# The last group's k load moves from ScalarE's DMA queue to SyncE's, in a fused attention and SwiGLU kernel

## The chip, the cores and the metric

The kernel runs on one core of one Trainium2 chip. The metric is the device time of one execution in microseconds (us). The engines are named as in the profile: PE (TensorE, with PEld its weight loads), DVE (VectorE), ACT (ScalarE), POOL (GpSimd) and SP (SyncE). SPq and ACTq are the DMA issues in the instruction streams of SP and ACT.

## The reference

A decayed linear attention over 4 batches, 8 heads, 768 positions and a head size of 64 is followed by a SwiGLU block of 512 by 1536. In short:

```python
for b in range(nb):                       # blocks of 64 positions
    intra = (qb @ kb.T * Dmask) @ vb      # per batch and head; Dmask = lam ** (i - j), causal
    inter = (qb * lam_pow) @ kv_state
    out[:, :, sl] = intra + inter
    kv_state = lam_block * kv_state + (kb * rev_pow).T @ vb
x = out.transpose(0, 2, 1, 3).reshape(B * S, H * D)      # 3072 x 512
result = (silu(x @ w_gate) * (x @ w_val)) @ w_out        # 3072 x 512
```

All inputs and the output are float32 in memory; the kernel multiplies in bfloat16.

## The kernel before, in words

The order of the work on every engine is written out by hand; there is no scheduler. The attention is cut into 12 groups (0 to 11), each of 256 positions of one batch with all heads. Two groups make one token tile `t` (0 to 5) for the SwiGLU block, so attention of later groups runs between the SwiGLU steps of earlier tiles. Groups 6 to 11 share one form, which matters here:

- `load_group(g)` loads k (`kraw`, four DMAs), q (`qraw`, four) and v (two DMAs), 512 KB each, in this order.
- `cast_scaled(g)` makes the bfloat16 tile `qk`: ACT casts k (L279), DVE multiplies q by its decay (L281), and then SP issues one transposing DMA from `qk` into `qkt` (L269), which waits for both.
- `v_scale(g)` multiplies v by its decay on POOL (L256), into `v_s`.
- `scores(g)` (PE L374, masks on DVE L379) needs `qkt`; `upd_mm(g)` (PE L406) needs `v_s` and `qk`; `inter` (L500) and `intra` (L513) make the attention output.
- `attend(g)` puts them together on PE: `inter(g)`, `upd_mm(g + 1)`, `scores(g + 1)`, `intra(g)`.

In the stage around the change, token tile 3 runs its SwiGLU steps (L564 gate on PE, silu on ACT L569, L582 value on PE, product on DVE L586). In step 6 of that tile the plan calls `cast_scaled(10)` and then `load_group(11)`. `attend(8)` and `attend(9)` follow steps 5 and 10. Then comes `out_units(2)`, the output projection of tile 2 (PE L802), which is made of seven products per half, in the order p1, p7, p6, p2, p5, p4, p3. ACT copies the result of p1 (L813) and p7 (L817) out, DVE adds (L827) what p6 left in a bank to the copy of p7, and p5 reuses that bank; after p5 DVE adds once more (L831), before p3 uses the bank again. A list of small jobs, handed out between the products by a fixed count, puts `cast_scaled(11)` behind p1 and four subtractions on DVE (`x_combo`, L693) behind p7, p2 and p5. `scores(11)` and `upd_mm(11)` come in the unit after it, `ffn_unit(4, 0)` (PE L712, DVE L754).

A load that ACT or SP issues stands in that engine's order like any other instruction: what is behind it in the stream waits until it is issued.

Of the kernel before, what the change touches and what calls it, by code (L numbers as in the profile page):

```python
# [19 lines left out]
@with_exitstack  # L20
def kernel(
    ctx: ExitStack,
    tc: tile.TileContext,
    q: bass.AP,
    k: bass.AP,
    v: bass.AP,
    lam: bass.AP,
    moe_w_gate: bass.AP,
    moe_w_val: bass.AP,
    moe_w_out: bass.AP,  # L30
    out: bass.AP,
):
    nc = tc.nc
    with tc.manual_schedule():
        _body(ctx, tc, nc, q, k, v, lam, moe_w_gate, moe_w_val, moe_w_out, out)


def _body(ctx, tc, nc, q, k, v, lam, moe_w_gate, moe_w_val, moe_w_out, out):
# [70 lines left out]
    def load_fp32(g, eng, src, what, h0=0, h1=H):  # L109
        if (what, g) not in st:  # L110
            st[(what, g)] = (v_pool if what == "v" else raw_pool).tile(
                [128, H, 2 * D], FP32, name=what, tag="v" if what == "v" else "raw")
        t = st[(what, g)]
        if g < NAT0:
            eng.dma_start(out=t[:, h0:h1], in_=gsrc(src, g, h0)[:, 0:h1 - h0])
            return
        b, i = groups[g]
        base = src.offset + b * H * S * D + i * 2 * BLK * D
        parts = [(0, 128, False)] if what == "v" else [(0, M, False), (M, M, True)]
        for s in range(2):  # L120
            for p0, n, rev in parts:
                eng.dma_start(
                    out=t[p0:p0 + n, :, s * D:s * D + D],
                    in_=bass.AP(tensor=src.tensor,
                                offset=base + (H - 1) * S * D * rev + (p0 + s * BLK) * D,
                                ap=[[D, n], [-S * D if rev else S * D, H], [1, D]]))
# [134 lines left out]
    def load_group(g, parts="kqv"):  # L261
        for src, what in ((k, "kraw"), (q, "qraw"), (v, "v")):
            if what[0] in parts:
                load_fp32(g, nc.scalar if what == "kraw" and g in KACT else nc.sync, src, what)

# [54 lines left out]
                        op=ALU.mult)  # L320


    KACT = (11,)
    later = []

    def run_later(n):
# [939 lines left out]
```

## Time and profile before

| what | value |
|---|---|
| median of 3 runs | 218.8 us (218.75 to 219.83) |
| the profiled execution | 219.09 us, span 217.3 us |
| granted PE clock | 1.00 |
| PE busy | 209.8 us, 97% of the span |
| DVE, ACT, POOL busy | 149.0, 129.0 and 91.5 us |
| k loads on SP | 28 issues (20 of 128 KB, 4 of 256 KB, 4 of 512 KB), 128 KB landing after 3.2 us (median) |
| k loads on ACT | 4 of 128 KB, 4.7 us |

The span runs from the first to the last instruction of one execution; the execution's own time is 1.8 us longer. Rows of a timeline give the start, the duration, the engine, the line, the operation with its output and inputs, the count, and in brackets the idle time before it with what ended it. In the chain of work that ended last each row is a start, a length and the work. The time to landing of a DMA is counted from the start of its issue. A releaser in brackets is inferred from semaphores; where the engine named had been done for long, it was another, often a DMA.

### The profile page before, as it was taken

To read this page: it belongs to the slowest core of one execution; us is meant where nothing else is said; L and a number is where in the kernel's file an instruction comes from. 1 tells how busy PE (TensorE), PEld (TensorE's weight loads), DVE (VectorE), ACT (ScalarE), POOL (GpSimd) and SP (SyncE) were. 2 spreads that over 40 slices of the span, in tenths; PEclk is the share of its full clock that TensorE was granted. 3 is DMA by queue.
4 is the path that set the end of the run, shared out by engine and by line. 5 is a ranking of instruction groups with operands and counts; after the bars stand their busy time and mean duration, and the time that the engine had idled before them with its cause. 6 is when DMAs were issued, how large, how long until landed. Compare 5 with 4: busy or idle time off the path is not lost.

```text
span 217.3 us, 6851 instructions
## 1 busy us (share of the span) xinstructions
PE 209.8 (97%) x2797; PEld 154.5 (71%) x2801; DVE 149.0 (69%) x267; ACT 129.0 (59%) x280; POOL 91.5 (42%) x126
## 2 busy tenths in 40 slices
PE   8879999999999999999999998999999999999994
PEld 3557455888887548866654544888888888888883
DVE  1763447576678799765387979896797379961760
ACT  6778577566545144638367566755882766646522
POOL 6675645927599050777852325410650022200200
PEclk9999999999999999999999999999999999999999
DMA  6999999999997877989779999572000400005014
GB/s 186 346 355 383 374 352 310 264 277 226 386 254 160 198 205 177 242 189 232 189 162 212 204 204 210 128 203 89 5 5 3 193 0 3 0 0 196 0 51 145
DMA packets 88320, 39.76 MB, mean 183 GB/s; under 512 B 57698, under 2 KB 83938, under 8 KB 88290
## 3 DMA queue, kind: packets, MB, share of 16 engines
q1 hardware_dynamic: 84978, 38.22, 65.8%
q10 hardware_dynamic: 3312, 1.11, 2.0%
q8 instruction: 22, 0.36, 0.7%
q14 instruction: 8, 0.07, 0.1%
HBM read 28.31 MB, written 6.29 MB: 159 GB/s over the span
## 4 chain that ended last, share of the span: by engine, by line
PE 90%; ACT 3%; DVE 2%; POOL 2%; issue 1%; POOLq 1%; DVEq 0%
PE bank L802 21%; PE bank L564 20%; PE bank L582 19%; PE bank L712 15%; PE bank L602 5%; PE bank L513 3%; PE bank L500 2%; PE bank L406 1%; PE bank L348 1%; DVE ssb L355 1%; PE bank L310 1%; POOL v_s L256 1%; PE bank L374 1%; PE bank L180 1%; ACT sil L739 1%
## 5 line engine op out<-in xcount | busy, mean ns | idle before, releaser
L586 DVE TENSOR_TENSOR h<-sil,bank 128x256 bf16<-128x256 bf16 (+1 forms) x67 | 35.0, 533 | 27.8 <-PE bank L582 20.5
L564 PE MATMUL bank<-xt,wg_sb 128*128 128x256 bf16 (+1 forms) x276 | 52.6, 315 | 0.0
L582 PE MATMUL bank<-xt,wv_sb 128*128 128x256 bf16 (+1 forms) x276 | 52.4, 314 | 0.0
L569 ACT ACTIVATE sil<-bank 128x256 bf16<-128x256 f32 (+1 forms) x67 | 31.7, 480 | 23.8 <-PE bank L564 19.7
L582 PEld LDWEIGHTS <-wv_sb 128*128 128x128 bf16 x276 | 26.9, 98 | 14.7
L564 PEld LDWEIGHTS <-wg_sb 128*128 128x128 bf16 x276 | 25.9, 98 | 13.4 <-DVE xt L525 0.2
L256 POOL TENSOR_TENSOR v_s<-v,dec 128x512 bf16<-128x512 f32 (+1 forms) x18 | 23.2, 1305 | 27.1 <-DMA v<-in_v_dram 13.9
L742 POOL TENSOR_TENSOR h<-sil,es 128x512 bf16<-128x512 bf16 x6 | 7.0, 1163 | 50.0 <-ACT sil L739 50.0
L802 PEld LDWEIGHTS <-h 128*128 128x128 bf16 x240 | 23.3, 98 | 3.4 <-issue 0.3
L802 PE MATMUL bank<-wo_sb,h 128*128 128x256 bf16 x180 | 21.6, 273 | 0.1
L802 PEld LDWEIGHTS <-hs 128*128 128x128 bf16 x180 | 17.6, 98 | 2.7
L355 DVE TENSOR_TENSOR ssb<-bank,causal 128x512 bf16<-128x512 f32 x24 | 15.4, 684 | 2.7 <-PE bank L348 2.7
L754 DVE TENSOR_TENSOR bank<-bank,es 128x512 f32<-128x512 f32 x12 | 7.8, 694 | 11.4 <-PE bank L712 10.1
L712 PEld LDWEIGHTS <-ws 128*128 128x128 bf16 x144 | 13.8, 97 | 2.3 <-issue 0.2
L802 PE MATMUL bank<-wt,hs 128*128 128x256 bf16 x120 | 15.0, 272 | 0.0
L739 ACT ACTIVATE sil<-bank 128x512 bf16<-128x512 f32 x18 | 10.7, 596 | 7.0 <-POOL h L742 4.6
L461 POOL TENSOR_TENSOR kvf<-kvs,ups 128x256 f32<-128x256 f32 x8 | 5.8, 726 | 19.5 <-ACT ups L428 19.5
L742 DVE TENSOR_TENSOR h<-sil,bank 128x512 bf16<-128x512 bf16 x18 | 12.2, 682 | 1.5 <-ACT sil L739 1.4
L712 PE MATMUL bank<-xs,ws 128*128 128x256 bf16 x96 | 12.8, 272 | 0.0
L525 ACT CAST xt<-bank 128x512 bf16<-128x512 f32 x19 | 11.6, 663 | 2.0 <-PE bank L513 1.5
L461 POOL TENSOR_TENSOR kvf<-kvf,ups 128x256 f32<-128x256 f32 x16 | 12.2, 763 | 0.9
L428 ACT COPY ups<-bank 128x256 f32<-128x256 f32 (+1 forms) x24 | 9.5, 451 | 2.5 <-PE bank L406 2.4
(119 smaller groups left out, 362.0 us busy)
## 6 DMA issues: line engine op xcount, KB each, us to landing
out_dram<-osb SPq DMA_DIRECT2D x22, 256.0 KB, 2.1
v<-in_v_dram SPq DMA_DIRECT2D x18, 256.0 KB, 4.6
woraw<-in_moe_w_out_dram SPq DMA_DIRECT2D x6, 512.0 KB, 8.6
qraw<-in_q_dram SPq DMA_DIRECT2D x24, 128.0 KB, 3.2
wraw<-in_moe_w_gate_dram SPq DMA_DIRECT2D x5, 512.0 KB, 7.4
wraw<-in_moe_w_val_dram SPq DMA_DIRECT2D x5, 512.0 KB, 7.0
kraw<-in_k_dram SPq DMA_DIRECT2D x20, 128.0 KB, 3.2
kraw<-in_k_dram SPq DMA_DIRECT2D x4, 512.0 KB, 6.6
```

What stands on the lines that cost most here:

```text
L256: eng.tensor_tensor(out=st[("vs", g)][:, h0:h1], in0=st[("v", g)][:, h0:h1].rearrange("p h (s d) -> p h s d", s=2), in1=vfac(g, h0, h1), o ...
L355: nc.vector.tensor_tensor(out=ssb[:, h2, 2 * c:2 * c + 2].rearrange("p a s n -> p a (s n)"), in0=sp[(c, h2)].rearrange("p (a x) -> p a x", ...
L461: nc.gpsimd.tensor_tensor(out=o, in0=f, in1=u, op=ALU.add)
L525: fns[r](out=xt[:, g % 2, :, r].rearrange("p h (m s) -> p h s m", s=2) if g < NAT0 else xt[:, g % 2, :, :, r * M:r * M + M], in_=op[r].rea ...
L564: nc.tensor.matmul(gp[:, n0:n1], wg_sb[:, mc, fs], xt[:, g0:g1, mc].rearrange("p g b n -> p g (b n)"), start=(mc == 0 and n0 == 0), stop=( ...
L569: nc.scalar.activation(sil[:, 0:N], gp[:, 0:N], AF.Silu)
L582: nc.tensor.matmul(vp[:, n0:n1], wv_sb[:, mc, fs], xt[:, g0:g1, mc].rearrange("p g b n -> p g (b n)"), start=(mc == 0 and n0 == 0), stop=( ...
L586: nc.vector.tensor_tensor(out=h_sb[:, fc % FH, b0:b1].rearrange("p b n -> p (b n)"), in0=sil[:, 0:N], in1=vp[:, 0:N], op=ALU.mult)
L712: nc.tensor.matmul(o[:, fi * 256:fi * 256 + 256], lhs(i, c, 2 * j + fi), rhs(c), start=(start and fi == 0 and c == 0), stop=(c == KH - 1), ...
L739: nc.scalar.activation(sil[key], src, AF.Silu)
L742: eng.tensor_tensor(out=h_of(half, r), in0=v3(sil[half, r]), in1=v3(src), op=ALU.mult)
L802: nc.tensor.matmul(o, lhs(f), rhs(f), start=(start and f == 0), stop=(f == FH - 1), skip_group_check=True)
```

## The change

`KACT` lists the groups whose k is issued from ACT. It held group 11 and becomes empty, so `load_group(11)` issues all ten DMAs of group 11 from SP. In SP's stream the four k DMAs now stand behind the transposing DMA of group 10, which `cast_scaled(10)` issued, and ahead of the q and v DMAs of group 11. ACT's stream loses four DMA issues, which stood behind its cast of k of group 10; the streams of PE, DVE and POOL keep their order.

```diff
-    KACT = (11,)
+    KACT = ()
```

The one place that reads it, in `load_group`:

```python
load_fp32(g, nc.scalar if what == "kraw" and g in KACT else nc.sync, src, what)
```

## The prediction

> **What bounds the kernel now.** I read the page first: TensorE (PE) is busy 97% of the span at a granted clock of 1.00 throughout, and the chain that ended last is 90% PE. Time can be won or lost only where PE waits. So I took the chain in order of time around group 11's load (126 to 150 us):
>
> ```profile
> 130.72 0.88 PE bank L564 x4
> 131.59 0.08 issue
> 131.67 2.24 POOL v_s L256 x2
> 133.91 0.04 issue
> 133.96 0.38 PE bank L406 x16
> ```
>
> The only foreign link there is GpSimd's `v_scale(10)`. PE's timeline shows what waits: the state update of group 10 (`upd_mm`, L406), against the same step one group earlier, which runs through:
>
> ```profile
> 122.59 0.36 PE L406 MATMUL bank<-v_s,qk 64*64 64x64 bf16 x20
> ...
> 132.77 0.26 PE L406 MATMUL bank<-v_s,qk 64*64 64x64 bf16 x8
> 133.96 0.38 PE L406 MATMUL bank<-v_s,qk 64*64 64x64 bf16 x16 [0.93 <-POOL v_s L256]
> ```
>
> What made GpSimd late stands in the timelines of SyncE's queue (first fence) and ScalarE (second):
>
> ```profile
> 103.78 1.69 SPq L269 DMA_TRANSPOSE qkt<-qk  x1
> ...
> 124.89 2.21 SPq L122 DMA_DIRECT2D v<-in_v_dram  x2
> 129.12 2.99 SPq L269 DMA_TRANSPOSE qkt<-qk  x1
> 132.16 2.66 SPq L122 DMA_DIRECT2D qraw<-in_q_dram  x4
> 134.92 1.20 SPq L122 DMA_DIRECT2D v<-in_v_dram  x2
> 140.36 1.65 SPq L269 DMA_TRANSPOSE qkt<-qk  x1
> ```
>
> ```profile
> 125.70 2.56 ACTq L122 DMA_DIRECT2D kraw<-in_k_dram  x3
> 128.36 1.08 ACT L569 ACTIVATE sil<-bank 128x512 bf16<-128x512 f32 x2 [1.76 <-PE bank L564]
> ```
>
> v of group 10 is issued at 124.89 and 126.49, in the same microseconds as the four k pieces of group 11 on ScalarE's queue (from 124.97). The DMA rows of v, asked one by one, give 5.5 and 5.0 us to landing for these two (so 131.5), and 4.4 us for group 11's second v. GpSimd starts 0.2 us after that landing; its label "PE bank L564" names work long done. The k pieces therefore delay v10. The VectorE (DVE) timeline then shows who needs the loads that the change puts later:
>
> ```profile
> 139.00 1.22 DVE L281 TENSOR_TENSOR qk<-qraw,qdn 128x1024 bf16<-128x1024 f32 x1
> 140.13 1.27 DVE L693 TENSOR_TENSOR xs<-xt 128x512 bf16<-128x512 bf16 x1
> 141.33 0.75 DVE L827 TENSOR_TENSOR bank<-bank,osb 128x256 f32<-128x256 f32 x2
> ...
> 142.52 0.41 DVE L693 TENSOR_TENSOR xs<-xt,xs 128x512 bf16<-128x512 bf16 x1
> ```
>
> L281 scales q11 without waiting. Behind it in order stand L693 and L827, and PE's product p5 of `out_units(2)`, at 141.83, writes the bank that L827 reads. That L827 ends about 141.70, so p5 has some 0.1 us to spare.
>
> **Removed: four issues on ScalarE, 2.7 us** (0.69 and 2.56). They hold ScalarE until 128.26 and two silus come 1.8 us late, but PE has no gap from 123.64 to 132.4. The bank ring covers them: 0.
>
> **Uncovered: v10 comes earlier.** Alone, its two issues take 0.6 each (rows of groups 9 and 11: 0.57 to 0.63), not 1.54. The second starts at 125.5 and lands 4.4 later (group 11's row; groups 6 to 9 show 3.8 to 5.3): 129.9. `v_scale(10)`, 2.23 us, ends at 132.2, before PE asks for it at 132.64. What that is worth: `attend(8)` takes 1.32 us from its first L500 at 122.32 to the next L564 at 123.64; `attend(9)` takes 2.48 (132.37 to 134.85). Difference: **-1.16 us**. The stall can pass to the next in line, the scores of group 10 (L374), which would start at 132.8 and need the transposes of group 10; these land at 134.1 now (129.12 + 5.0). They wait for DVE's L281 of group 10, which waits 0.8 us for q10; its last piece took 3.5 us to land, its first two 3.1. So their issue comes between 128.75 and 129.12; I take 128.9. Their time has two kinds of rows: 1.64 to 1.69 us of issue (78.33, 103.78, 140.36), and 2.73 to 2.99 (89.90, 116.62, 129.12). Before 103.78 the last transfer issued earlier landed 1.3 us after the transposes' start; before 89.90 and 129.12 it landed 3.1 and 3.2 us after (a store, and the last k at 127.66 + 4.7). With k gone, v10 lands some 1.0 us after the start, nearest to 103.78. I take that row: 1.69 of issue, 3.7 to landing, 132.6. The gain stands whole; with 5.0 to landing (133.9) only 0.1 of it is left.
>
> **Moved: k11 behind the transposes, q11 and v11 behind k11.** On SyncE's queue k11's four issues start 1.75 us after the transposes' start (103.78 to 105.53) and take 2.72, so 130.65 to 133.4; the fourth q issue starts 2.04 after the first: 128.9 + 1.75 + 2.72 + 2.04 = 135.4. The same issue now starts at 134.19 and lands 4.2 later; the last q of groups 7 to 10 took 3.2, 4.6, 3.1 and 3.5. I take its own row: q11 is in at **139.6**. DVE, drawn forward with PE, reaches L281 at 139.00 - 1.16 = 137.8 and waits 1.8 us. Then, from landing: 0.13 to start (as at 127.76), 1.13 for L281, 0.33 for L693, 0.37 for the first L827 and 0.1 to PE: p5 starts 2.06 after the landing, at 141.7, against 141.83 now. L693 is put at 0.33 because its 1.27 beside `v_scale(11)` (from 140.06) falls to 0.41 without it, and v11, issued until 138.0, lands after 141. The slow DVE work then falls on the next two L693, ahead of L831; p3 needs L831 4.7 us after q11's landing, and they end at most 4.6 after: 0.
>
> k11's last piece lands near 136.5, before ScalarE's cast at 137.4: 0. Group 11's transposes start about 0.7 us later than now and, at 3.7 to 5.0, land by 146.1; the scores of group 11 run at 147.60: 0. `v_scale(11)` moves from 140.06 to 141.3, used at 152.95: 0. SyncE's next stores wait for data until 144.39: 0.
>
> **Sum.** p5 at 141.7 for 141.83, and behind it PE is the bound to the end: -1.16 + 1.0 = **-0.16 us**. On the profiled 219.09 (span 217.3 and 1.8 around it) that is 218.9; that execution is 0.29 above the median of 218.8, so 218.6 there.
>
> The Trainium skill, "DMA: Bandwidth & Descriptors", section "Queues, rings and completion order", speaks against the change: on each DMA engine a queue's descriptors are consumed in ring order, and ScalarE's queue has a ring of its own. By it k11 can't begin under the transposes, as it could on ScalarE's ring; it names no duration.
>
> **The rivals.**
> *Whole gain*: q11's last piece takes 3.1 us instead of 4.2 and lands at 138.5; p5 is free at 140.6, in time for its advanced start at 140.7. For it: three of the five last-q rows are 3.1 to 3.5. Against: group 11's own 4.2, with the same v behind it. -1.16: 217.6.
> *Late queue, slower*: the transposes' issue stays at 2.99 from 129.12, so q11's fourth issue moves by k11's whole 2.72 to 136.9 and lands at 141.1; p5 starts at 143.2, +1.3 us whatever was won before: 220.1. It decides wherever q11 lands after 139.8. For it: v10 is still in flight when the transposes start, in twice as many pieces of half the size as a store's. Against: the backlog is shorter by 2 us. The same page's section "Issuing engines are not separate DMA queues" says that a second issuing engine saves only the sequencer's time to initiate; by it taking that engine away costs those 2.72 us of issue and wins no transfer rate.
> *Nothing moves*: v10's 5 us came from q10 ahead of it, not from k (group 9's second v took 5.3 without any k beside it), and q11 lands by 139.8: 218.8. Against: v10's first issue took 1.54 and k's third and fourth took 5.7 and 4.7 to land. That the k loads don't move at all is excluded: the built programs differ in these issues alone.
>
> **How the numbers follow.** Forecast 0.48 (-0.9 to +0.6), whole gain 0.14, late queue 0.28 (+0.6 to +2), nothing moves 0.10. About 0.5%, 1.1 us, is what a measurement of this kernel can tell from no change. Faster by that: 0.10 of the whole gain's 0.14. Slower: 0.22 of the late queue's 0.28. Same: 0.68. The range goes from the whole gain, 217.6, to the late queue, 220.2; the forecast's own is 217.9 to 219.4.
>
> **What would show it.** Right: the 0.93 in front of L406 gone, `v_scale(10)` from about 130, the transposes at 128.9 with 1.7 of issue, and a DVE wait of 1 to 2 us for q11 in front of L281, with a PE gap at p5 near 141. Wrong, if `v_scale(10)` still starts at 131.6 (k was not the cause), if PE waits for qkt instead of v_s, or if ScalarE stands at its cast of k11.

## The result, and the profile after

The changed kernel takes a little longer: a median of 219.97 us (218.57 to 223.62, 21 runs) against 218.43 us (217.62 to 219.83, 21 runs) of the kernel before, run in turn with it. The ratio is 1.0049, with a 95% interval of 1.0028 to 1.0070, which is 1.07 us; it leaves three disturbed, slower executions of the changed kernel out, and isn't the quotient of the two medians. The forecast was 0.16 us faster. The profiled execution took 219.38 us, where the one of before had taken 219.09.

The head of the page, and its queues, show that the loads moved and little else did. q10 is ScalarE's queue; it carried 3312 packets and 1.11 MB before:

```profile
span 217.7 us, 6854 instructions
...
q1 hardware_dynamic: 87090, 38.74, 65.8%
q10 hardware_dynamic: 1200, 0.59, 0.9%
```

SyncE's timeline, with start and duration in the first two columns, as in the prediction:

```profile
123.53 2.85 SPq L122 DMA_DIRECT2D v<-in_v_dram  x2
128.91 1.66 SPq L269 DMA_TRANSPOSE qkt<-qk  x1
130.61 2.69 SPq L122 DMA_DIRECT2D kraw<-in_k_dram  x4
133.35 3.67 SPq L122 DMA_DIRECT2D qraw<-in_q_dram  x4
137.12 1.18 SPq L122 DMA_DIRECT2D v<-in_v_dram  x2
```

PE is 0.54 us further ahead here: `attend(8)` begins at 121.78 and not at 122.32. The transposes of group 10 take 1.66 us to issue instead of 2.99; counted from `attend(8)`, they begin at 7.13 instead of 6.80. The k loads stand behind them, and the q loads, which began at 132.16 before, begin at 133.35 and take 3.67 us instead of 2.66. The two v issues of group 10 take 2.85 us, with no k on ScalarE's queue, where they had taken 2.21. GpSimd's timeline has `v_scale(10)` at 129.32, where it was at 131.67, and `v_scale(11)` at 141.96, where it was at 140.06:

```profile
129.32 2.50 POOL L256 TENSOR_TENSOR v_s<-v,dec 128x512 bf16<-128x512 f32 x2 [3.70 <-PE bank L564]
...
141.96 2.45 POOL L256 TENSOR_TENSOR v_s<-v,dec 128x512 bf16<-128x512 f32 x2 [6.39 <-DMA v<-in_v_dram]
```

PE's timeline shows one wait gone and one new:

```profile
132.08 0.42 PE L406 MATMUL bank<-v_s,qk 64*64 64x64 bf16 x24
132.62 0.45 PE L374 MATMUL bank<-qkt 64*64 64x64 bf16 x32
...
138.96 1.47 PE L802 MATMUL bank<-wo_sb,h 128*128 128x256 bf16 x12
141.71 1.47 PE L802 MATMUL bank<-wt,hs 128*128 128x256 bf16 x12 [1.28 <-DVE bank L827]
```

`upd_mm(10)` (L406) no longer stops in the middle, and the scores behind it (L374) wait for nothing. The product p5, the last row, now waits 1.28 us. In the kernel before it had followed p2 without a gap:

```profile
141.83 1.47 PE L802 MATMUL bank<-wt,hs 128*128 128x256 bf16 x12
```

Why it waits is read off the chain of waits, in order of time:

```profile
134.03 1.64 SPq L122
...
136.38 3.25 DMA qraw<-in_q_dram
...
139.76 0.10 DVE qk L281
...
140.90 0.42 DVE xs L693
141.32 0.35 DVE bank L827
...
141.71 4.09 PE bank L802 x36
```

The last piece of q11 is issued at 136.38 and lands 3.25 us later; L281, L693 and L827 follow in DVE's order, and then PE. That is the step that the prediction called the moved one.

A single pair of profiles is not enough here, since executions of one kernel differ by as much as the effect. So the experiments below include three further profiled executions of the kernel before and two of the changed one. All times count from the first L500 of `attend(8)`, except the second column, which is the length of `attend(9)` from its first L500 to the next L564. "End" runs from the issue of SyncE's last store to the end of the span.

| kernel | attend(9) | p5 starts | p3 starts | span ends | end |
|---|---|---|---|---|---|
| before, as predicted from | 2.48 | 19.51 | 22.13 | 94.97 | 2.56 |
| before, three more | 1.33, 2.07, 1.62 | 18.46, 19.09, 18.78 | 21.08, 21.71, 21.40 | 93.9, 94.6, 94.3 | 2.56 each |
| before, mean of four | 1.88 | 18.96 | 21.58 | 94.4 | 2.56 |
| after, three | 1.48, 1.41, 1.28 | 19.93, 19.47, 19.11 | 22.55, 22.41, 22.03 | 95.9, 95.7, 95.35 | 3.03, 3.03, 3.04 |
| after, mean of three | 1.39 | 19.50 | 22.33 | 95.65 | 3.03 |

### The profile page after: what moved, and what is told of

It is laid out like the page before. It is cut to its first block, busy times and chain, and to the rows that moved or that the text cites. A ratio compares the mean times of both kernels' runs of the same rounds, so it can differ in the third digit from the quotient of the medians.

```text
span 217.7 us, 6854 instructions
## 1 busy us (share of the span) xinstructions
PE 209.7 (96%) x2801; PEld 154.1 (71%) x2801; DVE 148.2 (68%) x267; ACT 129.4 (59%) x280; POOL 91.8 (42%) x126
## 4 chain that ended last, share of the span: by engine, by line
PE 78%; DMA 7%; SPq 5%; issue 2%; ACT 2%; DVE 2%; POOL 1%; POOLq 1%; DVEq 0%; ACTq 0%
PE bank L802 18%; PE bank L564 17%; PE bank L582 16%; PE bank L712 15%; PE bank L602 5%; DMA kraw<-in_k_dram 3%; SPq L122 3%; SPq L115 2%; DMA v<-in_v_dram 2%; PE bank L513 2%; PE bank L500 2%; DMA qraw<-in_q_dram 1%; PE bank L406 1%; POOL v_s L256 1%; ACT sil L739 1%
## 5 line engine op out<-in xcount | busy, mean ns | idle before, releaser
L586 DVE TENSOR_TENSOR h<-sil,bank 128x256 bf16<-128x256 bf16 (+1 forms) x67 | 35.1, 533 | 26.6 <-PE bank L582 19.6
L564 PE MATMUL bank<-xt,wg_sb 128*128 128x256 bf16 (+1 forms) x276 | 52.6, 315 | 0.0
L564 PEld LDWEIGHTS <-wg_sb 128*128 128x128 bf16 x276 | 26.0, 98 | 13.4 <-DVE xt L525 0.2
L461 POOL TENSOR_TENSOR kvf<-kvf,ups 128x256 f32<-128x256 f32 x16 | 13.1, 817 | 0.9
L835 ACT COPY osb<-bank 128x256 f32<-128x256 f32 x10 | 3.7, 373 | 12.6 <-PE bank L802 12.6
```

The source lines that it names most:

```text
L461: nc.gpsimd.tensor_tensor(out=o, in0=f, in1=u, op=ALU.add)
L564: nc.tensor.matmul(gp[:, n0:n1], wg_sb[:, mc, fs], xt[:, g0:g1, mc].rearrange("p g b n -> p g (b n)"), start=(mc == 0 and n0 == 0), stop=( ...
L586: nc.vector.tensor_tensor(out=h_sb[:, fc % FH, b0:b1].rearrange("p b n -> p (b n)"), in0=sil[:, 0:N], in1=vp[:, 0:N], op=ALU.mult)
```

## The experiments

The theory after the first look, as the expectations below have it: the stall of 1.16 us at `attend(9)` belongs to every execution of the kernel before; the wait of p5 for q11 is real, and hangs on L281's place in DVE's order; and the program's end costs about half a microsecond more because SyncE's stream holds four more DMAs. The rivals: the stall was long by chance in the one execution shown, q11 is not what p5 waits for, and the longer end is chance. The first part of the theory fell, the other two held.

### The changed kernel again, without an edit

> The changed kernel once more, for a second profiled execution. Theory: PE waits at p5 of the projection of tile 2 for DVE's L827, which stands behind the scaling of q11 (L281), and the size of this wait varies with q11's landing; p5 starts 19.9 us or more after the first L500 of attend(8) (19.5 in the kernel before), and from SP's last store issue to the end of the span it takes 3.0 us (2.6 before). Rival, chance: either of the two is not there again: p5 at 19.5 or the end at 2.6. Time against the kernel before: +0.6 to +1.5 us.

219.47 us (12 runs) against 218.85 (35 runs of before), ratio 1.0028 (0.9998 to 1.0057): +0.6 us, though the interval just takes in no change. The wait of p5 was there, 0.89 us, and "end" was 3.03 as expected. But p5 started at 19.47, below the expected 19.9 and where the rival had it, and p3 started another 0.3 late, for L831. A later execution:

> The changed kernel a third time. Theory: SyncE's issues behind the transposes of group 10 hold one that takes 1.2 to 1.7 us instead of 0.63 (among the fifth to seventh), the fourth q issue starts 7.0 to 7.5 us after the transposes, attend(9) takes 1.3 to 1.7 us, DVE waits 1 to 2.5 us for q11, p5 starts 19.4 to 20.0 us after attend(8)'s first L500, and SP's last six stores to the end take 10.5 to 10.6. Rival (the two executions seen were unlucky ones): no long issue, 6.5 us, p5 at 18.4 to 18.9.

p5 waited 0.63 us and started at 19.11, below what was expected. The long issue was there, but it was the shortest seen, 1.09 us, and the last of the eight; so the fourth q issue started only 6.47 us after the transposes. p3 was again 0.3 late. DVE's timeline of that execution shows where the 0.3 comes from:

```profile
142.05 1.16 DVE L693 TENSOR_TENSOR xt<-xt 128x512 bf16<-128x512 bf16 x1
143.14 1.26 DVE L693 TENSOR_TENSOR xs<-xt,xs 128x512 bf16<-128x512 bf16 x1
144.32 0.74 DVE L831 TENSOR_TENSOR osb<-bank,osb 128x256 f32<-128x256 f32 x2
```

Both L693 lie beside `v_scale(11)`, which ran from 141.88 to 144.11, and take 1.16 and 1.26 us; without it they take 0.41 (last such row of the prediction). L831 stands behind them, and p3 waits for it.

### The kernel before again, without an edit

> The kernel before once more, for a second profiled execution. Theory (the 1.16 us at attend(9) belongs to that kernel, since k11 on ScalarE's queue delays v10): attend(9) takes 2.2 us or more from its first L500 to the next gate product, with a wait of L406 for v_s. Rival (v10's late landing was that execution's alone): attend(9) takes 1.3 to 1.6, v_scale(10) starts before 9.0 us after attend(8)'s first L500, and the removed wait was worth nothing in most executions. p5 at 19.5 by the first and 18.3 to 18.7 by the second; last six stores to the end 10.1 by both.

> The kernel before a third time, to see how often attend(9) waits. Same two readings: 2.2 us or more at attend(9) with a wait for v_s (theory), or 1.3 to 1.6 (rival).

> The kernel before a fourth time. v of group 10 lands 6.2 to 6.7 us after its first issue (with k11 on ScalarE's queue beside it), and what attend(9) takes depends on when that first issue falls: with the issue 1.6 us after attend(8)'s first L500 or less 1.3 to 1.45, with 2.5 us 2.0 to 2.5; p5 between 18.4 and 19.6.

The times were 217.78, 218.33 and 218.81 us. The expectation that the stall is a fixed part of the kernel fell with the first of them. PE's timeline, and under it GpSimd's:

```profile
132.54 0.42 PE L406 MATMUL bank<-v_s,qk 64*64 64x64 bf16 x24
```

```profile
129.94 2.26 POOL L256 TENSOR_TENSOR v_s<-v,dec 128x512 bf16<-128x512 f32 x2 [4.04 <-DMA v<-in_v_dram]
```

Here all 24 matmuls of L406 run in 0.42 us. v10 landed early enough although the k pieces were on ScalarE's queue as always, since SyncE had issued the first v piece 1.58 us after `attend(8)` began and not 2.57. In the other two it was issued at 2.49 and 2.35, and `attend(9)` took 2.07 and 1.62 us. From that issue to the start of `v_scale(10)` the four executions show 6.78, 6.24, 6.40 and 6.13 us. The sum of both is when `v_scale(10)` starts after `attend(8)`, and the stall follows it: 9.35, 7.82, 8.89 and 8.48 us, with 2.48, 1.33, 2.07 and 1.62 us for `attend(9)`. How late v10 is counts for PE only by this sum, and SyncE's offset against PE is a part of it.

### The cast behind p2, in the changed kernel

Here `cast_scaled(11)`, and so L281, stands two jobs further back on DVE, behind the two subtractions and the L827 that p5 needs:

```diff
     trickle[:] = [y for z in TR2 for y in xw[z]]
+    trickle[0:3] = [trickle[1], trickle[2], trickle[0]]
```

> The changed kernel with cast_scaled(11) handed out behind p2 instead of p1, so that DVE's L827 no longer stands behind the scaling of q11. Theory (q11 through DVE's order is what p5 waits for): the wait in front of p5 goes, the 0.93 in front of L406 stays gone, p5 starts 18.4 us after attend(8)'s first L500, and the time is the kernel before's minus 1.2 plus up to 0.5 for the end of the program: -0.6 us, from -1.2 to 0. Rival (what is late is k11 at ScalarE's cast, or the transposes of group 11): a wait of about the same 1.3 us appears at the scores of group 11 or at ScalarE's copies, and the time stays at +0.6 to +1.5 us.

218.71 us (12 runs), ratio 1.0016 (0.9985 to 1.0048). The profiled execution has no wait at p5, which started at 18.68, and p3 at 21.30. DVE's row of L281 and PE's row of p5:

```profile
141.58 1.22 DVE L281 TENSOR_TENSOR qk<-qraw,qdn 128x1024 bf16<-128x1024 f32 x1
```

```profile
142.28 1.47 PE L802 MATMUL bank<-wt,hs 128*128 128x256 bf16 x12
```

L281 is the same work with the same q11, and p5 follows p2 without a gap. So it was L281's place ahead of L827 that handed q11's lateness on to p5. "End" stayed at 3.04.

The gain of 0.6 us that was expected did not come: the ratio allows -0.3 to +1.05 us. Counted from `attend(8)`, the profiled span ended at 94.6, 1.0 earlier than the mean of the changed kernel and 0.2 later than the mean of before. p3 started 0.28 earlier than before, and the longer end took that back. The scores of group 10 waited 0.32 us for their transposes here, which the changed kernel's own three executions do not show. (The execution itself took 219.92 us, 1.2 above its median; most of that arose ahead of `attend(8)`, which began at 123.6.)

### The same edit in the kernel before

> The kernel before with the same move of cast_scaled(11), k11 still on ScalarE's queue. Theory: q11 was no wait there, so nothing is won: the 0.93 in front of L406 stays, p5 at 19.5 us after attend(8)'s first L500, time 0 (within 0.3 us). Rival (the late cast is a gain by itself, by freeing DVE ahead of p5): -0.5 us or more here too.

219.19 us, ratio 1.0020 (0.9993 to 1.0047); `attend(9)` 1.41, p5 18.51, span end 94.0, "end" 2.56. The expected stall at `attend(9)` was not there, which is another miss of the theory that it is fixed: v10 was issued at 1.57 and took 5.49 us in this execution. The times show no gain from the edit where q11 comes early.

### Four small DMAs in the kernel before

The kernel before, with four DMAs of 32 bytes into a tile that nobody reads, on SyncE behind `out_units(2)`. They lengthen SyncE's stream as the change does, and load nothing of weight:

```diff
     out_units(2, many=list(M2))
+    for c in range(4):
+        nc.sync.dma_start(out=pad[0:1, c * H:(c + 1) * H],
+                          in_=bass.AP(tensor=lam.tensor, offset=lam.offset, ap=[[0, 1], [1, H]]))
```

> The kernel before with four more DMAs of 32 bytes in SyncE's stream (into an unused tile), issued where SyncE is idle, so that its stream is as long as in the changed kernel. Theory (the end of the program grows with SyncE's stream): SP's last store issue to the end of the span takes 3.0 us instead of 2.6, and the time is +0.4 to +0.5 us. Rival (the longer end in the changed kernel's profile was chance, or comes from the load itself): 2.6 us, time 0 within 0.2 us.

"End" rose from 2.56 to 3.03, the value of the changed kernel. The last six stores of the kernel before, of the changed one and of this one, in SyncE's timelines:

```profile
207.21 7.86 SPq L808 DMA_DIRECT2D out_dram<-osb  x6
```

```profile
207.11 7.86 SPq L808 DMA_DIRECT2D out_dram<-osb  x6
```

```profile
207.48 7.85 SPq L808 DMA_DIRECT2D out_dram<-osb  x6
```

The stores take the same 7.86 us. From the first of them the span runs on for 10.08 (217.29), 10.56 (217.67) and 10.5 us (218.0). The time was 219.64 us, ratio 1.0028 (0.9993 to 1.0063): in line with half a microsecond, but the interval takes in no change. Nor can its span be used alone, since PE lost 0.8 us ahead of `attend(9)` in that execution, most of it waiting for DVE's L586.

With two DMAs instead of four:

> The kernel before with two more DMAs of 32 bytes in SyncE's stream (four gave 10.5 from the first of the last six stores to the end). If the end grows with each instruction: 10.3. If it is a step at some length of the stream: 10.1 or 10.5.

"End" was 2.47, so the step lies between two and four more DMAs and isn't a price for each. `attend(9)` took 2.48 in this execution, with 0.93 us in front of L406: the long stall does recur. SyncE was not especially late here, with v10's first issue at 2.12, but v10 took 7.19 us, so `v_scale(10)` again started at 9.31.

### Late cast, and a SyncE stream as short as before

The edit of the cast, and the four stores of tile 2 moved from SyncE to ScalarE:

```diff
-        def store(g, r, c0, c1, eng=nc.sync if t >= SY else nc.scalar):
+        def store(g, r, c0, c1, eng=nc.scalar if t == 2 else nc.sync if t >= SY else nc.scalar):
```

> The changed kernel with cast_scaled(11) behind p2, as tried alone, and the four stores of tile 2 issued by ScalarE, which makes SyncE's stream as short as in the kernel before. Theory: no wait at p5 (18.4 to 18.7 us after attend(8)'s first L500) and the program's end back at 10.1 us from the first of SP's last six stores (10.5 to 10.6 with the four issues on SyncE), so from attend(8) to the end of the span 94.2 us or less (95.0 before, 95.9 and 95.7 in the changed kernel); time against the kernel before -0.4 us, from -1 to +0.2. Rival (the end depends on something else than SyncE's stream): 10.5 stays, 94.6.

Half of it held. There was no wait at p5 (18.49), and "end" was back at 2.56 with k of group 11 on SyncE, which shows from the other side that the number of DMAs in SyncE's stream sets it. But the time was 219.99 us, ratio 1.0051 (1.0021 to 1.0082), instead of a gain. PE's timeline has a new wait at the scores of group 11:

```profile
147.26 0.45 PE L374 MATMUL bank<-qkt 64*64 64x64 bf16 x32 [0.78 <-DMA qkt<-qk]
```

The transposes of group 11 were issued at 142.31 and took 4.9 us to land. That takes back 0.78 us. The profiled execution, 218.87 us, ended at 94.8, only 0.4 behind the mean of before; its time is the lowest of its 12 runs, and where the median lost the rest is not shown.

### q11 ahead of k11

In the changed kernel, group 11 alone:

```diff
-        for src, what in ((k, "kraw"), (q, "qraw"), (v, "v")):
+        for src, what in ((q, "qraw"), (k, "kraw"), (v, "v")) if g == 11 else ((k, "kraw"), (q, "qraw"), (v, "v")):
```

> The changed kernel with q11 ahead of k11 in SyncE's queue, both behind the transposes of group 10. Theory (what counts is the last of the loads that cast_scaled(11) takes, since both casts stand ahead of p5's inputs in their engines' order): DVE's wait for q11 falls to 0.5 us or less, ScalarE waits 1.5 to 2.5 us for k11 at its cast, the copies of p7 (L817) stand behind that cast, and PE waits at p5 as long as or longer than now: p5 at 19.9 to 20.6 us after attend(8)'s first L500. Rival (only q's landing counts): p5 at 18.4 to 18.9 and no wait.

One run, 220.49 us. L281 didn't wait for q11, and the expected wait at p5 did not come. ScalarE stood at its cast of k11 instead, for less than the 1.5 to 2.5 us expected:

```profile
140.28 1.05 ACT L279 CAST qk<-kraw 128x1024 bf16<-128x1024 f32 x1 [0.79 <-DMA kraw<-in_k_dram]
```

p5 started at 20.48, inside the range expected, but by luck: PE had waited 0.96 and 0.83 us for DVE's L586 ahead of `attend(9)`, where the order of q11 and k11 had not acted yet. For the same reason what this order is worth can't be read from the run.

### k11 on SyncE, ahead of the transposes

`load_group(11)` leaves its k out, and `load_group(10)` ends with it:

```diff
-                load_fp32(g, nc.scalar if what == "kraw" and g in KACT else nc.sync, src, what)
+                if not (g == 11 and what == "kraw"):
+                    load_fp32(g, nc.sync, src, what)
+        if g == 10:
+            load_fp32(11, nc.sync, k, "kraw")
```

> k11 on SyncE's queue, but ahead of the transposes of group 10 (behind v10). Theory (a load's place in SyncE's one queue decides, not that SyncE issues it): q11's place behind the transposes is the one it has in the kernel before, so its fourth issue starts 5.0 to 6.0 us after the transposes and p5 doesn't wait for it; v10 lands within 5.7 us of its first issue and L406 doesn't wait; the price moves to the transposes, which are issued up to 1.5 us later and land at 12.0 us or later after attend(8)'s first L500, so PE waits for qkt at the scores of group 10, 0.5 to 2 us. Rival (any k on SyncE's queue makes q11 late): DVE waits 1 us or more for q11. The end is 10.5 in both.

One run, 220.95 us, with before at 220.16 beside it. q11 came in time for p5, its fourth issue only 4.39 us behind the start of the transposes, but `attend(9)` took 3.43 us, with PE waiting for the transposes of group 10 (its lines stand three further on; L377 is the scores):

```profile
132.89 0.71 PE L409 MATMUL bank<-v_s,qk 64*64 64x64 bf16 x24
135.38 0.45 PE L377 MATMUL bank<-qkt 64*64 64x64 bf16 x32 [1.77 <-DMA qkt<-qk]
```

They were issued 8.33 us after `attend(8)`, against 7.13 in the changed kernel, behind the 2.76 us that the four k issues held SyncE. With one queue, PE paid in both orders: with k11 ahead of the transposes it waited for these, and with k11 behind them for q11, which stands behind k11. v10 took 5.60 us here. Over all executions, from v10's first issue to `v_scale(10)`: 6.13 to 7.19, mean 6.4, in the seven with k11 on ScalarE's queue (but for 5.49 in one of them), and 5.05 to 5.79, mean 5.4, in the seven with it on SyncE. The transfer beside it thus costs v10 about 1.0 us on average. One of v10's two issues is mostly a long one, in either kernel; where it was the second, v10 took 6.24 to 6.68 with k on ScalarE's queue (three executions) and 5.05 to 5.79 with it on SyncE's (five). Where neither was long, it took 5.49 and 5.34, one execution each, so the price is not the same every time. The Trainium skill, "DMA: Bandwidth & Descriptors", section "Issuing engines are not separate DMA queues", says that DMAs of all issuing engines share the same 16 engines and interleave; the 6.4 against 5.4 agrees with that.

## Why the prediction was wrong, point by point

Its sum was -1.16 (the stall) + 1.0 (p5) = -0.16 us. The means of the table and of PE's waits give, for the same path: -0.49 (the stall) + 0.93 (p5) + 0.1 (steps between) + 0.2 (p3) + 0.47 (the end) = +1.2 us. Timing gave +1.07, and +0.6 in the second comparison. By term:

- **Uncovered: v10 comes earlier.** This is the first step that failed, by its size. That v10 is earlier without k beside it was right: `v_scale(10)` was forecast from about 130, 7.7 us after `attend(8)`, and came 7.54, 7.18 and 7.36 after it; the 0.93 in front of L406 was gone in all three executions. But the 1.16 was the stall of one execution, and that was the longest of four. The mean of `attend(9)` was 1.88, not 2.48, and the gain 1.88 - 1.39 = 0.49 us; with the two versions of each kernel whose edits act only later, and where PE lost nothing before it, the means are 1.90 and 1.46. The row itself could not tell this. It could have been doubted from the issue time of v, which depends on how far SyncE is behind PE, but no second execution was there to show its spread. One of the step's reasons was wrong as well: the long issue of v10 (1.54 us instead of 0.6) does not need k. Without k on ScalarE's queue its two issues took 2.85, 1.21 and 2.30 us, and what got shorter is the way to landing. SyncE's timeline of before had such a row for group 6, while nothing was issued on ScalarE's queue:

```profile
71.96 2.09 SPq L122 DMA_DIRECT2D v<-in_v_dram  x2
```

- **Moved: q11 behind k11.** The wait of p5 was forecast as 1.03 (141.7 less the advanced 140.67; 1.0 in its sum) and measured as 1.28, 0.89 and 0.63, mean 0.93. Counted from `attend(8)`, p5 was forecast at 141.7 - 122.32 = 19.38 and came at 19.50 on average. That is near by luck, since errors cancelled in it. The transposes were forecast 6.58 after `attend(8)` and came 7.13, 7.05 and 6.93 after. The fourth q issue was forecast 6.51 us after the start of the transposes and came 7.47, 7.36 and 6.47 after: one of the eight issues behind the transposes takes 1.1 to 1.6 us instead of 0.63 (the 1.64 in the chain above; in the third execution it is the last q issue itself, and delays only what follows). Against that, the landing took 3.25, 2.99 and 3.63 us, not 4.2. SyncE's timeline of before had the long issue in group 9, behind the transposes of 103.78 whose 1.69 the prediction took over. It left this row aside, and took 2.04 us from the first to the fourth q issue:

```profile
108.26 3.68 SPq L122 DMA_DIRECT2D qraw<-in_q_dram  x4
```

- **L831 and p3, put at 0.** The step had the two slow L693 end 4.6 us after q11's landing and p3 due at 4.7, and left out L831 itself, which stands between them: 0.37 for its first half and 0.1 to PE. In the third execution, whose L693 are shown above, q11 was in at 139.78, the second L693 ended 4.62 later, and p3 started 5.0 later. Where both L693 were slowed, in two of three executions, p3 was 0.32 and 0.3 late. The Trainium skill, "SBUF — State Buffer", section "Who interferes with whom", says that VectorE and GpSimd share a port pair under an exclusive lock; the 1.16 and 1.26 us against 0.41 agree with it.
- **PE is the bound to the end.** This is the second step that failed. The prediction carried p5's delay unchanged to the end of the span. It said nothing on the end of the program, and 0.47 us arose there, behind the last store. This was the term that was absent, and it is about as large as the whole gain.
- **The other terms put at 0** cost PE nothing: it did not wait for the transposes of group 10 or of group 11, and `v_scale(11)`, forecast for 141.3, came at 141.96, 141.34 and 141.88. But k11 was not always in ahead of ScalarE's cast, which the prediction had named as a sign of being wrong: the cast (L279) waited 0, 0.52 and 0.40 us for it. DVE's L827 stood behind L281 for longer than that, so nothing came of it at PE.

Of the rivals, the late queue has the right sign and, with 220.1, nearly the median, but not by its own way: its premise, transposes that stay at 2.99 us of issue, was not seen in any execution of the changed kernel (1.66 in all three), nor its 1.3 us more at p5.

Left open: what SyncE does in the added 0.47 us; why one of the issues behind the transposes is long; and the part of the late-cast, short-stream version's loss that its profile does not show. No version here was shown to beat the kernel before.

## What to carry to other kernels

A stall read from one profile is one draw: before its removal is booked as a gain, ask what its length depends on, and where that is the offset between two engines' streams or the landing time of a load, look at a second execution or book part of it. A row that is taken over as a model should be taken over with the rows behind it in the same stream. A load taken off a second queue frees the transfers beside it, but its issue time is paid by every load behind it on the queue that it joins, so look for who needs the last of those. A margin of a tenth of a microsecond, on an engine whose work slows beside another's, should be priced to the last instruction and not put at zero.

## What the runs showed of the hardware

- From SyncE's last store to the end of the span took 2.56 us in six executions with the stream of before, 2.47 in the one with two more DMAs in it, and 2.97 to 3.04 in all seven with four more, whether these load 512 KB or 128 bytes.
- Behind a transposing DMA that took 1.7 us to issue, one of the next eight DMA issues took 1.1 to 1.6 us where the others took 0.63, in each of the three executions of the changed kernel; behind the transposes of group 9 it was so in all four of the kernel before (1.65, 1.21, 1.56 and 1.40 us).
- The 512 KB of v took 6.4 us to be in with k issued on another queue at the same time, and 5.4 without (means of seven executions each; one pair differed by only 0.15).
